# One-core attention with a feed-forward block: step order, PSUM banks and instruction ranks read from stored tables

## The chip, the core and the metric

The kernel runs on one core of one Trainium2 chip. A core has TensorE (PE, matmuls and transposes), VectorE (DVE), ScalarE (ACT), GpSimd (POOL) and SyncE (SP, which here issues every DMA). Matmul results land in PSUM, eight banks, from where DVE and ACT read them. The metric is the device time of one execution in microseconds (us); of several runs the median counts.

## What is computed

Batch 4, 8 heads, 768 positions, head size 64; model width 512, inner width 2048. All inputs are float32 in memory.

```python
k_sum = k.reshape(B, H, nb, 32, D).max(axis=3)            # 24 blocks of 32 keys
v_sum = v.reshape(B, H, nb, 32, D).mean(axis=3)
scores_l = scale * q @ k.T, kept where |i - j| < 16, else -1e9
scores_s = scale * q @ k_sum.T + log(32)
a = softmax(concat([scores_l, scores_s]))                 # with 1e-9 on the sum
x = a @ concat([v, v_sum])                                # heads side by side: [B, S, 512]
xn = (x - mean) / sqrt(var + 1e-6) * g_ln
out = x + relu(xn @ w_ch1) @ w_ch2
```

## The kernel before

The 3072 rows are cut into 24 tiles of 128. A tile's attention is done in two half steps of four heads each (t = 0 to 47). The first 12 half steps (batch 0) work on float32 data: `early_qk` makes scores (tile name `s`), `softmax` takes on DVE the masked scores with their minimum (`p`, `mn`) and on ACT the exponentials, `early_transp` transposes on PE (`pp`, copied to `pT`), `early_pv` multiplies by the values (`o`). Later half steps work on pairs of fp16 numbers. `ln` and `lnT` normalize and transpose a tile (`xn`, `xs`).

The feed-forward part runs on pairs of tiles (groups of 256 rows), each float32 product split into three fp16 ones. Its 32 weight blocks of 512 KB each are fetched (`fetch_w`, tile `raw`), decoded on DVE by three instructions (`dec_w`: `wf<-raw`, `wf<-raw,wf`, `raw<-raw,wf`), squared and summed on ACT, scaled by a common power of two per set of blocks (`scale_w`, six times: a tiny matmul, tile `wps`, sums over partitions) and split into fp16 halves on ACT and DVE (`conv_w`, tile `wp`). Only then can `g1` (12 matmuls a piece into `h`, then `hh` on ACT and `hl` on DVE) and `g2` (6 matmuls a piece into `a`) use them. From row group 5 on, `sp1`, `sp2` and `sw2` do the same by a scheme with fewer products (tiles `qx`, `qy`, `qz`, `a_x`, `a_y`).

For batches 1 to 3, statistics are loaded through a few staging buffers (`bst`, `qs`, `qw`): `batch_k` (block maxima `kmax`), `batch_q`, `batch_v` (block sums `vsum`); each buffer is loaded, reduced on DVE, reduced on ACT and then loaded again.

Nothing is issued while the steps are called. A `Plan` records each operation with what it must wait for, then `issue` (line 439) orders all 3593 recorded operations by a list scheduler with built-in costs (`schedule`, line 300, `improve`, `search`) and writes them out engine by engine. Lines 457 and 460 are where every instruction of the trace is issued, so tiles rather than lines tell them apart. Three things settle the order before: the order in which the body calls the steps decides who uses a rotating buffer first; `LOADS` (line 64) fixes the first DMA issues on SP by hand; PSUM tiles alternate between the two banks of their kind (`psum`, line 475: kinds s, o, h, a). Where the scheduler expects PE to wait long, it puts transposes of the identity there as fill (`spare`).

Of the kernel before, what the change touches and what calls it, by code (L numbers as in the profile page):

```python
# [104 lines left out]
class Plan:  # L105
# [12 lines left out]
    def __init__(self):  # L118
        self.ops, self.slots, self.prev, self.uses = [], {}, {}, {}
        self.joined, self.opens, self.closes = False, None, ()  # L120
        self.names, self.stage = [("", ())], 0
        for e in self.ENGINES:
            setattr(self, e, Plan.Queue(self, e))
# [7 lines left out]

    def step(self, f):


        def call(*a):
            outer, self.stage = self.stage, len(self.names)
            self.names.append((f.__name__, a))
            f(*a)
            self.stage = outer

        return call

# [296 lines left out]
    def issue(self, nc):  # L439
        for x in self.ops:  # L440
            x.first = in_front(self.names[x.stage], x.engine)
        self.watch()
        after = [self.waits(x) for x in self.ops]
        then = [[] for _ in after]
        for i, x in enumerate(after):
            for j, wait in x:
                then[j].append((i, wait))
        rank = [0.0] * len(after)
        for i in reversed(range(len(after))):
            x = self.ops[i]  # L450
            rank[i] = min((rank[j] for j, _ in then[i]), default=0.0) - x.busy - x.moving - self.WAIT[x.engine]
        best = self.search(rank, after, then)
# [12 lines left out]
def body(ctx: ExitStack, tc, qt, qa, qe, kt, ks, va, vb, vs, g_ln, w1, w2, blocks, out):  # L465
# [3 lines left out]
    pools = {n: ctx.enter_context(tc.tile_pool(name="ps" + n, bufs=1, space=bass.MemoryType.PSUM)) for n in "soha"}  # L469
    banks = dict.fromkeys("soha", 0)  # L470

# [92 lines left out]

    turn = {}

    def home(kind):
        n = turn[kind] = turn.get(kind, -1) + 1
        return HOMES[kind][n % len(HOMES[kind])]

    stg_n = [0]

    def stg(tag, shape, dt=F32):
        stg_n[0] += 1
        if tag == "bst1":
            tag = ("bst", "qs")[stg_n[0] % 2]
        elif tag in ("bst", "qs"):
            tag = home(tag)
        return work(tag, f"{tag}{stg_n[0]}", shape, dt, 1 + (tag == "xn"))

# [3 lines left out]
    @pl.step  # L584
    def batch_k(b, hp):
        if hp == 0:
            bt["m", b] = work("kmax" if b else "ksum", f"kmax{b}", [P, 4, NB], F32, 1 + (b == 0))
            if b:
                bt["a", b] = work("vabs", f"vabs{b}", [P, 3, 8])
                nc.gpsimd.memset(bt["a", b][:], 0.0)  # L590
        m = bt["m", b]
        n = 2 if b else 1
        for c in range(n):
            cs = slice(NB // n * c, NB // n * (c + 1))
            if b:
                kk = stg("bst1" if b == 1 else "bst", [P, NB // n, BLK])[:]
# [55 lines left out]
    def batch_v(b, c):  # L652
        if c == 0:
            bt["v", b] = work("vsum", f"vsum{b}", [96, P], F32, 1)
        t, ab = bt["v", b], bt["a", b]
        vv = stg("bst1" if b == 1 else "bst", [96, 16, BLK])
        nc.sync.dma_start(vv[:], vs[b, c])
# [5 lines left out]
    @pl.step  # L663
    def batch_q(b, c):
        x = stg("bst1" if b == 1 else "bst", [P, DM])
        nc.sync.dma_start(x[:], qa[b, :, c * DM : c * DM + DM])
        nc.scalar.activation(x[:], x[:], AF.Abs, accum_out=bt["a", b][:, 1, c : c + 1])
# [43 lines left out]
    def load_q(t):  # L711

        T, hh = divmod(t, 2)
        qs = stg('qs', [P, 4, P])
        for half in range(2):
# [8 lines left out]
    def load_k(t, pr):  # L724
        T, hh = divmod(t, 2)
        b = T // NT
        at = home("ksg")
        ksg = late[at] if at in late else work(at, f"ksg{t}_{pr}", [P, 2, NC])
# [3 lines left out]
        )  # L732
        at = home("kh")
        kh = work(at, f"kh{t}_{pr}", [P, 2, NC], F16) if at else late["kh"]
# [64 lines left out]
    def transp(t):  # L799

        p = st[t, "p"]
        p16 = work(home("p16"), f"p16_{t}", [P, 4, 3, P], F16)
        first, rest, last = (p16[:, :, i] for i in range(3))
# [3 lines left out]
        nc.gpsimd.tensor_tensor(last[:, :, D:], p[:, :, P:], last[:, :, :D], ALU.subtract)  # L807
        pT = work(home("pT"), f"pT_{t}", [P, 12, P], F16)
        nc.sync.dma_start_transpose(pT[:], p16.rearrange("p j i k -> p (j i k)"))
# [120 lines left out]
    def ln(T):  # L930
# [7 lines left out]
        nc.gpsimd.tensor_tensor(rs[:], rs[:], mhalf[:], ALU.pow)  # L938
        xn = stg("xn", [P, DM])
        if XA <= T < XE:  # L940
# [190 lines left out]
    def combine2(u):  # L1131

        top, low = (wt[2, rows2(u, j)] for j in range(2))
        yt, yb = (stg("xn", [P, DM]) for _ in range(2))
        for y, w in ((yt, top), (yb, low)):
# [317 lines left out]
    for t in range(8, 2 * TT + 1):  # L1453
# [30 lines left out]
        if t % 2:  # L1484
            norm(t // 2)
    with tc.manual_schedule():
        pl.issue(tc.nc)
# [54 lines left out]
```

## Time and profile before

| | |
|---|---|
| median of 3 runs | 611.51 us (608.76 to 613.46) |
| span of the profiled execution | 609.7 us |
| PE busy | 592.2 us, 97% |
| DVE busy | 520.5 us, 85% |
| ACT busy | 434.9 us, 71% |
| POOL busy | 235.9 us, 39% |
| DMA queue of SP | 95.04 MB, 63.3% of 16 engines |
| chain that ended last | PE 74%, DVE 14%, DMA 6% |

Matmuls are pipelined, so a PE that counts as busy may hide short waits; the spacing of matmul starts tells more. The shares are averages over stages with different limits, so the stretches have to be read one by one. Idle time of an engine that nothing waits for costs nothing.

### The profile page before, as it was taken

What the parts mean: (1) busy time and instruction counts of PE and PEld (TensorE: products, weight loads), DVE (VectorE), ACT (ScalarE), POOL (GpSimd) and SP (SyncE); (2) the same over time, 40 slices, a digit from 0 to 9 for tenths busy, and PEclk for the clock granted to TensorE, in tenths of its full rate; (3) what the DMA queues carried; (4) which work ended last, traced back from release to release, by engine and by line L of the source; (5) the groups of instructions that cost most, each with busy time, mean ns of one, the idle gap of its engine ahead of it and who ended that gap; (6) DMA issues with size and microseconds to landing.
All of it is one profiled execution on the core that took longest, in us unless ns stands there. A gap on an engine that the chain in (4) does not pass through costs nothing.

```text
span 609.7 us, 16537 instructions
## 1 busy us (share of the span) xinstructions
PE 592.2 (97%) x6097; PEld 448.4 (74%) x6097; DVE 520.5 (85%) x1351; ACT 434.9 (71%) x968; POOL 235.9 (39%) x447
## 2 busy tenths in 40 slices
PE   6998899989999999999999999999999999999997
PEld 4687776675677688677687867877685896987976
DVE  3799998899989989998999978678999999868435
ACT  2798798778889877669698857657867777544221
POOL 5131221123856675575354433317553532410000
PEclk8999999999999999999999999999999999999999
DMA  9990478624899995578899868736446673531101
GB/s 260 366 329 15 124 236 298 206 66 122 215 260 234 206 193 147 120 148 194 189 212 231 190 142 172 140 88 152 107 114 138 144 178 73 103 75 34 47 1 35
DMA packets 138176, 96.09 MB, mean 158 GB/s; under 512 B 96112, under 2 KB 120944, under 8 KB 138096
## 3 DMA queue, kind: packets, MB, share of 16 engines
q1 hardware_dynamic: 138096, 95.04, 63.3%
q8 instruction: 48, 0.79, 0.6%
q14 instruction: 32, 0.26, 0.1%
HBM read 66.27 MB, written 6.29 MB: 119 GB/s over the span
## 4 chain that ended last, share of the span: by engine, by line
PE 74%; DVE 14%; DMA 6%; ACT 2%; issue 2%; POOL 1%; SPq 0%; ACTq 0%; DVEq 0%; POOLq 0%
PE a L460 30%; PE qx L460 11%; PE h L460 11%; PE qz L460 6%; PE o L460 4%; PE s L460 4%; PE qy L460 3%; DVE wf L460 3%; PE a_x L460 3%; PE a_y L460 2%; DVE wp L460 2%; DVE raw L460 2%; DVE hl L460 2%; DVE p L460 1%; DMA k<-in_ks 1%
## 5 line engine op out<-in xcount | busy, mean ns | idle before, releaser
L460 PE MATMUL a<-wp,hh 128*128 128x512 f16 x640 | 190.4, 379 | 0.0
L460 PEld LDWEIGHTS <-wp 128*128 128x128 f16 x1968 | 152.0, 98 | 19.1 <-issue 2.0
L460 PE MATMUL a<-wp,hl 128*128 128x512 f16 x320 | 121.3, 379 | 0.0
L460 PE MATMUL h<-xs,wp 128*128 128x256 f16 x960 | 112.4, 273 | 0.4 <-DVE xs L460 0.4
L460 PEld LDWEIGHTS <-hh 128*128 128x128 f16 x736 | 68.9, 98 | 56.9 <-issue 0.2
L460 POOL TENSOR_TENSOR p<-p,p 128x512 f16<-128x512 f32 x72 | 75.8, 1058 | 61.0 <-ACT p L460 37.6
L460 PEld LDWEIGHTS <-wd 128*128 128x128 f16 x1176 | 70.7, 98 | 5.5
L460 ACT ACTIVATE p<-p,mn,sv 128x184 f32<-128x184 f32 x144 | 67.4, 529 | 7.7 <-POOL mn L460 7.5
L460 PEld LDWEIGHTS <-hl 128*128 128x128 f16 x368 | 36.0, 98 | 39.1 <-DVE hl L460 0.8
L460 POOL TENSOR_SCALAR mn<-mn,sv 128x2 f32<-128x2 f32 x72 | 33.2, 464 | 58.8 <-DVE mn L460 57.7
L460 DVE CUSTOM_DVE_ANT_0 p<-s,mask 128x184 f32<-128x184 f32 x144 | 43.1, 340 | 5.0 <-PE s L460 4.5
L460 PE MATMUL qx<-xs,wp 128*128 128x128 f16 x672 | 42.9, 219 | 0.1
L460 POOL TENSOR_SCALAR rs<-mv 128x1 f32<-128x1 f32 x24 | 8.9, 372 | 64.7 <-DVE mv L460 60.7
L460 ACT ACTIVATE v<-vst,sv 128x512 f16<-128x512 f32 x36 | 25.8, 719 | 11.2 <-PE o L460 9.6
L460 DVE SCALAR_TENSOR_TENSOR x<-a,wsc,x 128x512 f32<-128x512 f32 x40 | 29.7, 742 | 4.7 <-PE a L460 4.6
L460 ACT CAST p<-p 128x512 f16<-128x512 f32 x72 | 33.4, 506 | 0.2
L460 DVE SCALAR_TENSOR_TENSOR v<-vst,sv,v 128x512 f16<-128x512 f32 x36 | 31.4, 873 | 1.6 <-ACT v L460 1.6
L460 DVE SCALAR_TENSOR_TENSOR hl<-h,hh 128x512 f16<-128x512 f32 x40 | 27.0, 681 | 3.8 <-ACT hh L460 3.7
L460 ACT ACTIVATE hh<-h 128x512 f16<-128x512 f32 x40 | 23.5, 586 | 8.2 <-PE h L460 8.1
L460 PEld LDWEIGHTS <-pT 128*128 128x128 f16 x720 | 26.0, 98 | 2.5
L460 PE MATMUL o<-v,pT 128*128 128x65 f16 (+1 forms) x720 | 27.7, 193 | 0.0
L460 PEld LDWEIGHTS <-qhl 128*128 128x128 f16 x288 | 23.5, 98 | 3.3
(235 smaller groups left out, 1355.5 us busy)
## 6 DMA issues: line engine op xcount, KB each, us to landing
raw<-in_w SPq DMA_DIRECT2D x32, 512.0 KB
ksg<-in_kt SPq DMA_DIRECT2D x48, 184.0 KB
out_x<-x SPq DMA_DIRECT2D x20, 256.0 KB
qw<-in_qt SPq DMA_DIRECT2D x36, 128.0 KB
vst<-in_va SPq DMA_DIRECT2D x36, 128.0 KB
qs<-in_qt SPq DMA_DIRECT2D x36, 128.0 KB
keys<-in_kt SPq DMA_DIRECT2D x24, 184.0 KB
vst<-in_vb SPq DMA_DIRECT2D x80, 32.0 KB
```

The lines of the kernel that those rows point to most:

```text
L460: getattr(getattr(nc, self.ops[i].engine), op)(*a, **k)
```

## The change

No operation is added or removed: the same 3593 operations are recorded. What changes is what decides their order and their place.

- `step` now only collects calls; `record_steps` records them in the order of the stored table `ORDER` (621 steps), so rotating buffers may be taken in another order.
- `psum` takes the bank of each tile from `BANKS`, one digit for one of all eight banks, instead of alternating within a kind.
- `issue` takes one rank per operation from `RANKS` and runs the scheduler once with them; the search over starts is left out. `LOADS` is empty.
- Buffers that were chosen by a running count (`home`, `stg`) are now chosen by the number of the load (`stage_in`, `rows`).

```diff
+ORDER = (
+    "#)#&#,#'#7$Z###($e#+#9#;#:#<#%#D#3#8#-$k$[$l#5#6#$#4$c$h#1#2#*#=#>#?#@#A#W#B#C#l#E#F#X#G#H#I#J#K#L$f$]$_$v#M#N"
...
+BANKS = (
...
+RANKS = (
...
+LOADS = []
...
     def step(self, f):
+        return lambda *a: self.steps.append((f, a))
+
+    def record_steps(self):
+        order = decode(ORDER) or range(len(self.steps))
+        assert len(order) == len(self.steps)
+        for i in order:
+            f, a = self.steps[i]
+            self.stage = len(self.names)
             self.names.append((f.__name__, a))
             f(*a)
...
+        rank = decode(RANKS)
+        if not rank:
...
+        else:
+            best = self.improve(rank, after, then, 1)[0]
...
     def psum(tag, name, shape, at=None):
-        if at is None:
+        if BANKS:
+            tag, at = "s0s1o0o1h0h1a0a1"[2 * int(BANKS[len(turns)]) :][:2]
+            turns.append(at)
+        elif at is None:
             at = banks[tag] = 1 - banks[tag]
...
+    def stage_in(b, n, shape):
+        tag = home("bst", n) if b > 1 else ("qs", "bst")[n % 2]
+        return work(tag, f"in{b}_{n}", shape)
```

Where the rows stand is what the tables decide. The first place is SP's queue, from the last of the four key loads on (`k_3`; `qw` is a query tile, `vw` and `vend` values, `vst` value tails, `blk` and `gcol` constants, `raw` a weight block of 512 KB). Before:

```order
L460 DMA k_3_93<-in_ks 128x768
L460 DMA blk<-in_blocks 128x144
L460 DMA vw_100<-in_va 128x4x128 x2
L460 DMA vw_101<-in_va 128x4x128 x2
L460 DMA vw_102<-in_va 128x4x128 x2
L460 DMA vend<-in_vb 32x2x256
L460 DMA vst_77<-in_vb 32x2x128 x2
L460 DMA raw_252<-in_w 128x1024
L460 DMA raw_253<-in_w 128x1024
L460 DMA qw_95<-in_qe 128x512
L460 DMA raw_254<-in_w 128x1024
```

The same place after the change:

```order
L561 DMA k_3_93<-in_ks 128x768
L561 DMA qw_94<-in_qe 128x512
L561 DMA vw_100<-in_va 128x4x128
L561 DMA blk<-in_blocks 128x144
L561 DMA raw_112<-in_w 128x1024
L561 DMA vw_102<-in_va 128x4x128
L561 DMA qw_95<-in_qe 128x512
L561 DMA vw_100<-in_va 128x4x128
L561 DMA gcol<-in_g_ln 128x4x1
L561 DMA raw_128<-in_w 128x1024
L561 DMA raw_129<-in_w 128x1024
L561 DMA raw_107<-in_w 128x1024
```

The first weight block moved from behind all seven value loads to behind one of them, and three more blocks stand where one stood.

The second place is PE, from the end of the first scores on (`v` sums the value blocks of batch 0, `s_0` and `s_1` are the scores of the next half step, `pp` the transposes of the first one's probabilities). Before:

```order
L460 MATMUL s_1_111<-kx,qw_94 128x192
L460 MATMUL v_109<-vw_100,blk 120x512 x2
L460 MATMUL s_0_120<-ident 128x128
L460 MATMUL s_0_120<-kx,qw_94 128x184
L460 MATMUL s_1_121<-kx,qw_94 128x184
L460 MATMUL s_0_120<-kx,qw_94 128x192
L460 MATMUL s_1_121<-kx,qw_94 128x192
L460 MATMUL v_109<-vw_101,blk 120x512 x2
L460 MATMUL v_109<-vw_102,blk 120x512 x2
L460 MATMUL v_109<-vend,blk 120x512
L460 MATMUL pp_0_113<-ident,p 128x128 x3
```

After the change, from the second half step's last scores on (`qw_95` belongs to half steps 2 and 3):

```order
L561 MATMUL s_1_132<-kx,qw_94 128x192
L561 MATMUL pp_0_120<-ident,p 128x128 x3
L561 MATMUL pp_1_123<-ident,p 128x128 x3
L561 MATMUL s_0_146<-ident 128x128
L561 MATMUL s_0_146<-kx,qw_95 128x184
L561 MATMUL s_1_147<-kx,qw_95 128x184
L561 MATMUL s_0_146<-kx,qw_95 128x192
L561 MATMUL s_1_147<-kx,qw_95 128x192
L561 MATMUL pp_0_134<-ident,p_89 128x128 x3
L561 MATMUL v_116<-vw_100,blk 120x512
```

The scores of half steps 1 and 2 now stand ahead of the first value product instead of behind two and seven of them. Of the 70 fill transposes before (35 of them behind half step 5, the others later), 28 are left, all between the second and the third value product.

On DVE, the first instruction that decodes the first weight block moved ahead of the second half step's masked scores, and the sixth `wps` matmul, which is the last of its kind in both orders, stands behind 269 DVE instructions that it needs instead of 285.

## Rows read from the trace of the kernel before

**Rows 1.** The page: busy time of each engine, share of the span, instructions.
```profile
PE 592.2 (97%) x6097; PEld 448.4 (74%) x6097; DVE 520.5 (85%) x1351; ACT 434.9 (71%) x968; POOL 235.9 (39%) x447
```

**Rows 2.** 20 us stretches: us busy of PE, PEld, DVE, ACT, POOL; clock, DMA, GB/s.
```profile
20.00:40.00 20.00, 19.39 (x158) 16.11 (x157) 17.52 (x71) 18.71 (x52) 3.90 (x16) 1.00 1.03 386
40.00:60.00 20.00, 17.08 (x146) 14.77 (x147) 19.83 (x57) 17.12 (x47) 4.91 (x11) 1.00 0.24 72
...
140.00:160.00 20.00, 20.00 (x121) 11.42 (x119) 19.68 (x52) 18.84 (x41) 10.08 (x19) 1.00 0.55 155
```

**Rows 3.** Longer stretches, same columns.
```profile
0.00:140.00 140.00, 126.21 (x936) 96.35 (x937) 119.89 (x347) 106.86 (x293) 34.99 (x115) 0.99 0.65 211
140.00:300.00 160.00, 160.00 (x1396) 113.20 (x1394) 148.83 (x389) 131.63 (x282) 98.56 (x154) 1.00 0.81 184
```

**Rows 4.** Instructions on PE in order: start us, length us, what, [idle before <-releaser].
```profile
7.55 0.91 PE L460 MATMUL s<-kx,qw 64*128 64x184 f32 x8
11.66 3.63 PE L460 MATMUL v<-vw,blk 128*120 128x512 f32 x4 [3.21 <-DVE mn L460]
...
15.33 0.91 PE L460 MATMUL s<-kx,qw 64*128 64x184 f32 x8
16.17 3.69 PE L460 MATMUL v<-vw,blk 128*120 128x512 f32 x8
...
134.84 0.34 PE L460 MATMUL wps<-wacc,ones 128*128 128x8 f32 x2
...
606.25 0.27 PE L460 MATMUL a_x<-lone,hl 128*128 128x256 f16 x1
```

**Rows 5.** Instructions on DVE in order of time, same columns.
```profile
10.38 0.35 DVE L460 CUSTOM_DVE_ANT_0 p<-s,emask 128x192 f32<-128x192 f32 x1
...
16.39 0.36 DVE L460 CUSTOM_DVE_ANT_0 p<-s,emask 128x192 f32<-128x192 f32 x1 [4.84 <-PE s L460]
...
17.66 0.43 DVE L460 TENSOR_SCALAR wf<-raw 128x512 uint32<-128x512 uint32 x1
...
19.46 0.42 DVE L460 TENSOR_SCALAR wf<-raw 128x512 uint32<-128x512 uint32 x1
...
22.80 0.35 DVE L460 CUSTOM_DVE_ANT_0 p<-s,msk 128x184 f32<-128x184 f32 x1 [1.46 <-PE s L460]
...
104.17 0.68 DVE L460 TENSOR_REDUCE vsum<-qs 96x16 f32<-96x512 f32 x1 [1.68 <-DMA qs<-in_vs]
...
110.08 0.68 DVE L460 TENSOR_REDUCE vsum<-qs 96x16 f32<-96x512 f32 x1
```

**Rows 6.** The first weight loads on SP's queue, same columns.
```profile
12.41 0.89 SPq L460 DMA_DIRECT2D raw<-in_w  x2
```

**Rows 7.** The fill transposes: count, ns min/median/max, first and last start.
```profile
L457 PE MATMUL spare<-ident x69: 272/273/305, 41.7 to 71.6; 128*128 128x128 f32 x69
```

**Rows 8.** DVE's waits between 72 and 135 us: us in total, times, longest.
```profile
DVE vsum L460 <- DMA qs<-in_vs: 1.7, 1, 1.7
DVE vsum L460 <- DMA bst<-in_vs: 1.4, 1, 1.4
```

**Rows 9.** The stretches around PE's first wait, columns as in the 20 us stretches.
```profile
8.00:12.00 4.00, 0.80 (x7) 0.53 (x5) 3.00 (x10) 2.28 (x8) 1.45 (x15) 0.95 1.18 308
12.00:16.00 4.00, 4.00 (x13) 1.59 (x12) 0.00 (x0) 0.25 (x1) 0.00 (x0) 0.62 1.11 279
```

**Rows 10.** DVE between 140 and 300 us by form: busy us, mean ns | idle before.
```profile
L460 DVE SCALAR_TENSOR_TENSOR kl<-keys,sv,kh 128x368 f16<-128x368 f32 x11 | 9.1, 824 | 0.1
...
L460 DVE SCALAR_TENSOR_TENSOR kl<-ksg,sv,kh 128x368 f16<-128x368 f32 x11 | 7.0, 634 | 0.5 <-PE s L460 0.5
```

**Rows 11.** PE's waits between 140 and 606 us: us in total, times, longest.
```profile
PE a_y L460 <- DVE hl L460: 0.5, 1, 0.5
```

**Rows 12.** DVE up to 140 us by form: busy us, mean ns | idle before.
```profile
L460 DVE SCALAR_TENSOR_TENSOR hl<-h,hh 128x512 f16<-128x512 f32 x15 | 10.1, 681 | 0.0
...
L460 DVE TENSOR_REDUCE kmax<-bst 128x12 f32<-128x384 f32 x6 | 3.3, 543 | 0.0
```

More of the change, by code (lines that the diff above doesn't have):

```diff
@@ L57, with decode @@
+def decode(text):
+    n = [ord(c) - 35 - (c > "\\") for c in text]
+    return [90 * a + b for a, b in zip(n[::2], n[1::2])]
 SEQ = [(1 + m // 8 % 2, m % 8 + m // 16 * 8) for m in range(2 * NF)]
@@ L120, in __init__ @@
         self.joined, self.opens, self.closes = False, None, ()
-        self.names, self.stage = [("", ())], 0
+        self.names, self.stage, self.steps = [("", ())], 0, []
         for e in self.ENGINES:
@@ L447, in issue @@
                 then[j].append((i, wait))
[L448 to L452, printed above, removed]
+        rank = decode(RANKS)
+        if not rank:
+            rank = [0.0] * len(after)
+            for i in reversed(range(len(after))):
+                x = self.ops[i]
+                rank[i] = min((rank[j] for j, _ in then[i]), default=0.0) - x.busy - x.moving - self.WAIT[x.engine]
+            best = self.search(rank, after, then)
+        else:
+            best = self.improve(rank, after, then, 1)[0]
         self.time, self.start, self.end, fills = best
@@ L469, in body @@
     pools = {n: ctx.enter_context(tc.tile_pool(name="ps" + n, bufs=1, space=bass.MemoryType.PSUM)) for n in "soha"}
-    banks = dict.fromkeys("soha", 0)
+    banks, turns = dict.fromkeys("soha", 0), []
     def work(tag, name, shape, dt=F32, bufs=1):
@@ L563, in go_late, with home, rows @@
         late["kh"] = room[:, DM : DM + NC].bitcast(F16).rearrange("p (u c) -> p u c", u=2)
-    turn = {}
-    def home(kind):
-        n = turn[kind] = turn.get(kind, -1) + 1
+    def home(kind, n):
         return HOMES[kind][n % len(HOMES[kind])]
[L571 to L579, printed above, removed]
+    def stage_in(b, n, shape):
+        tag = home("bst", n) if b > 1 else ("qs", "bst")[n % 2]
+        return work(tag, f"in{b}_{n}", shape)
+    def rows(name):
+        return work("xn", name, [P, DM], F32, 2)
     bt = {}
@@ L595, in batch_k @@
             if b:
-                kk = stg("bst1" if b == 1 else "bst", [P, NB // n, BLK])[:]
+                kk = stage_in(b, 2 * hp + c, [P, NB // n, BLK])[:]
                 nc.sync.dma_start(kk, ks[b, hp, :, cs])
@@ L655, in batch_v @@
         t, ab = bt["v", b], bt["a", b]
-        vv = stg("bst1" if b == 1 else "bst", [96, 16, BLK])
+        vv = stage_in(b, 14 + c, [96, 16, BLK])
         nc.sync.dma_start(vv[:], vs[b, c])
@@ L664, in batch_q @@
     def batch_q(b, c):
-        x = stg("bst1" if b == 1 else "bst", [P, DM])
+        x = stage_in(b, 8 + c, [P, DM])
         nc.sync.dma_start(x[:], qa[b, :, c * DM : c * DM + DM])
@@ L713, in load_q @@
         T, hh = divmod(t, 2)
-        qs = stg('qs', [P, 4, P])
+        qs = work(home("qs", t), f"qs{t}", [P, 4, P])
         for half in range(2):
@@ L801, in transp @@
         p = st[t, "p"]
-        p16 = work(home("p16"), f"p16_{t}", [P, 4, 3, P], F16)
+        p16 = work(home("p16", t), f"p16_{t}", [P, 4, 3, P], F16)
         first, rest, last = (p16[:, :, i] for i in range(3))
@@ L807, in transp @@
         nc.gpsimd.tensor_tensor(last[:, :, D:], p[:, :, P:], last[:, :, :D], ALU.subtract)
[L808 removed]
+        pT = work(home("pT", t), f"pT_{t}", [P, 12, P], F16)
         nc.sync.dma_start_transpose(pT[:], p16.rearrange("p j i k -> p (j i k)"))
@@ L938, in ln @@
         nc.gpsimd.tensor_tensor(rs[:], rs[:], mhalf[:], ALU.pow)
-        xn = stg("xn", [P, DM])
+        xn = rows(f"xn{T}")
         if XA <= T < XE:
@@ L1133, in combine2 @@
         top, low = (wt[2, rows2(u, j)] for j in range(2))
-        yt, yb = (stg("xn", [P, DM]) for _ in range(2))
+        yt, yb = (rows(f"y{u}{n}") for n in "tb")
         for y, w in ((yt, top), (yb, low)):
```

96 lines of the change are left out of this document (89 added, 7 removed).

## The prediction, made before the changed kernel was run

> **What bounds the kernel now.** The busy line of the page comes first [rows 1]: PE is busy 97% of the span, so whatever an order can win is among the other 3% and what the busy time hides. The stretches say where that is. Up to 140 us PE is busy 126.2 of 140 us; from 140 to 300 us it is busy 160 of 160 [rows 3], and between 140 and 606 us its list of waits has one entry, of 0.5 us [rows 11]. So there are two kernels: one of 140 us with holes on PE, and one of 470 us in which PE never stops and in which an order can win almost nothing. The reader should look only at the first.
>
> In that part PE is not what limits. DVE is busy 19.8 of 20 us between 40 and 60 us, while PE is busy 17.1 [rows 2], and even that holds 69 transposes that only fill time, between 41.7 and 71.6 us [rows 7] (one more opens the fill). DVE decodes and splits 32 weight blocks there beside its attention work, and PE waits for what it makes. But DVE itself starts late. It takes the first half step's scores at 10.38 us, then waits 4.84 us for the second's, decodes the first weight block only at 17.66 us, and waits 1.46 us more for the third's scores at 22.80 us [rows 5]. The rows on PE say why: behind the first scores stands the value product `v`, which waits and then takes 3.63 us for four passes, and the second scores, though only 0.91 us long, come behind it, at 15.33 us; five more value products (3.69 us for the first eight passes) stand ahead of the third [rows 4]. The decoding is late because the first two weight loads are issued at 12.41 us [rows 6], behind all the values.
>
> So I measure the kernel at one landmark, the sixth and last `wps` matmul, at 134.84 us. The last matmul starts at 606.25 us [rows 4], 471.4 us later, of which about 1.1 are waits (the 0.5 listed, the rest hidden in the busy time). What comes behind, 3.4 us to the end of the span of 609.7 us, is a store that both kernels end with. Whatever the landmark gains, the span gains, if PE stays without holes.
>
> **The change, part by part.** No operation is added or taken away, so each term is an instruction that stands elsewhere.
>
> 1. *Work ahead of the landmark on PE.* I counted it from the order. Before: 29 pieces of `g1`, 14 of `g2`, 24 `pp`, 24 `o`, 12 `s` and the seven value products. After: the same, but 16 of `g2`, 22 `pp`, 22 `o`, 11 `s`. At the spacing of starts (1.3 us a piece, 0.33, 0.7, 0.84) that is +2.6 -0.7 -1.4 -0.8: 0.3 us less, nothing. PE does the same by then. The fill falls from 70 to 28 transposes, but a fill stands where PE would wait anyhow, so I cost it at nothing: it is the wait's length that counts, and that is DVE's.
>
> 2. *Work ahead of the landmark on DVE.* Before, 285 instructions lie ahead of the last one it needs; after, 269. Behind it now: four masked scores (0.27 us each in a row), two `kmax` of the next batch (0.46), two `vsum` (0.6), two `hl` (0.6), one normalization's statistics (0.6) and six short ones (0.5 in all); one more 0.66 us addition stands ahead. A row is about 0.08 us longer than the spacing, since neighbours overlap [rows 12]. Sum: 1.1 + 0.9 + 1.2 + 1.2 + 0.6 + 0.5 - 0.7 = **4.8 us less** (of 114 before). DVE has to do them later, behind the landmark, where it has 11 idle us in 160 [rows 3].
>
> 3. *DVE's start.* The second half step's scores now stand ahead of every value product, and the first weight load behind one value load instead of seven. Bounds: if both are always there in time, DVE loses none of the 4.84, 1.46 and the 0.4 us of small gaps up to 22.80: 6.7 us gained. [...] DMA should keep up: by the shapes in the order, 2.7 MB are asked for up to the first weight block where it was 4.1, and the queue moves 0.3 to 0.4 MB a us [rows 2, 9], so that block is there 4 us earlier, near 13 us, and each of the next (0.52 MB, 1.4 to 1.7 us) about as fast as DVE decodes one (1.8 us, 17.66 to 19.46 [rows 5]). I take **4.5 us**, nearer to the full gain than to none, because DVE has decoding to do whenever scores are late.
>
> 4. *Staging buffers.* Batch 1's statistics pass through two buffers, and DVE waited 1.7 and 1.4 us for their loads [rows 8]. One round (reduce, ACT, load again) took 5.9 us, 104.17 to 110.08 [rows 5]. After the change the last five rounds of each buffer are 5.1 to 5.7 us of DVE work apart, where most were 5.6 to 7.3: up to 5 x 0.8 = 4 us of waits in place of 3.1. Bounds: 2 us gained (ACT is quicker, 71% busy) to 5 lost. I take **1 lost**.
>
> 5. *Behind the landmark.* A few pieces later the new order needs DVE results with 1.5 us less PE work in front of them than at the landmark (a `g1` piece behind 111.8 us of DVE work, 109.5 of PE work with fill). Before, that difference did not grow. **1.5 lost.** The 0.5 us wait of `a_y` [rows 11] goes, since another group's piece now stands there; I leave as much for new waits among 470 us of PE work whose banks have all moved: nothing, bounds 0.5 gained to 3 lost.
>
> 6. *Banks and buffers.* A tile may take any of eight banks. Where PE waits for DVE that gives nothing; it is what lets steps 2 and 3 stand so. Nothing of its own.
>
> Sum: 4.8 + 4.5 - 1.0 - 1.5 = 6.8 us, so the landmark comes at about 128 us and the span is **602.9 us**. The profiled execution (609.7 us) lies a little under the median of the runs (611.51 us); in proportion that makes **604.5 us**.
>
> **The rivals.**
>
> *PE's clock stays low at the start.* [...] Time: 609.7 - 6.8 + 2.5 = 605.4, or 607 us as a median. Chance 0.15.
>
> *The staging buffers take it back.* Step 4 at 5 lost and step 3 at 2: 609.7 - (4.8 + 2 - 5 - 1.5) = 609.4, as a median 611. Against it: DVE has other work to put between. Chance 0.15. That the tables do nothing at all is out: the order shows the moves.
>
> *Everything in time.* Steps 3 and 4 at their good ends: 4.8 + 6.7 + 2 - 1.5 = 12, a span of 597.7, as a median 599.5. For it: each piece alone fits. Chance 0.14.
>
> *Slower: DVE becomes the bound after 140 us.* At 140 us of PE work DVE stood 5.4 us ahead of need by work count, and stands 1.6 ahead after the change: 3.8 us of reserve gone. Between 140 and 300 us DVE is idle 11.2 us [rows 3], and the 32 `kl` vary by source, 634 against 824 ns [rows 10]. If none of the idle time can be squeezed and all `kl` take 0.19 us more, 11.2 + 6.1 - 3.8 = 13.5 us of PE waits arise, 6.7 us more than is gained: a span of 616.4, a median of 618. It decides from 3.8 us on. Against it: most of that idle time is DVE waiting for ACT and PE because it is early. [...] Chance 0.08.
>
> **How the numbers follow.** Forecast 0.48 (600.5 to 608.5 by itself), then 0.15, 0.15, 0.14, 0.08. The range leaves out the last and the outer parts of two others: 598 to 612 us. One per cent, about what a measurement of this kernel can tell from no change, is 6.1 us: faster is below 605.4, slower above 617.6. Faster: 0.14, most of the forecast (0.38) and a little of the clock's case (0.04), 0.56. Slower: 0.08. Within: 0.36.
>
> **What would show it.** The second half step's scores start near 12 us and DVE's first `wf<-raw` near 12 to 13 us instead of 17.66: step 3. The sixth `wps` near 128 us, PE's spacing solid from there: steps 2 and 5. Waits of `vsum` or `kmax` on `bst` and `qs` above 4 us: step 4 too small. A clock under 1 beyond 16 us: the first rival. The forecast falls if PE's list of waits between 140 and 606 us, now 0.5 us, is several us long.

## The result, and the profile after

The changed kernel takes 606.86 us (median of ten runs, 602.15 to 612.93) against 611.03 us (608.76 to 613.46) of the kernel before on the same chip. The ratio is 0.9906, with a 95% interval of 0.9878 to 0.9934; it leaves out the run of 612.93 us, which was disturbed; the mean of the other nine is 605.5 us. So the change gains 0.7 to 1.2%, about 5.7 us. The profiled execution spans 604.7 us, 5.0 less than before; 6.8 were forecast.

The page of the changed kernel: busy time of each engine, its share of the span, instructions. PE loses 4.1 us of busy time [rows 1], which the 42 fill transposes fewer account for, roughly (27 in a row take 3.11 us, so 42 some 4.8 by estimate); DVE's share rises.

```profile
PE 588.1 (97%) x6055; PEld 446.3 (74%) x6055; DVE 523.9 (87%) x1351; ACT 435.7 (72%) x968; POOL 231.8 (38%) x447
```

Stretches of the changed kernel, then two of the kernel before, cut at each one's landmark, the sixth `wps` matmul: length, us busy of PE, PEld, DVE, ACT, POOL, granted clock, DMA share, GB/s.

```profile
0.00:40.00 40.00, 33.76 (x208) 25.96 (x209) 30.29 (x98) 26.41 (x73) 14.13 (x68) 0.91 0.99 339
40.00:126.31 86.31, 82.99 (x641) 63.45 (x640) 81.54 (x219) 73.86 (x200) 12.82 (x35) 1.00 0.52 169
140.00:300.00 160.00, 158.48 (x1360) 110.94 (x1359) 151.20 (x395) 134.14 (x298) 99.30 (x156) 1.00 0.83 200
```

```profile
0.00:40.00 40.00, 34.37 (x224) 25.79 (x224) 26.04 (x101) 24.98 (x69) 12.54 (x69) 0.96 0.99 331
40.00:134.84 94.84, 86.73 (x679) 67.24 (x679) 89.70 (x234) 80.21 (x220) 20.28 (x43) 1.00 0.52 165
```

These four rows up to the landmark hold the gain. By 40 us DVE has done 30.29 us of work where it had done 26.04: a start 4.2 us better. Up to the landmark it has 30.29 + 81.54 = 111.8 us to do where it was 115.7: 3.9 less. Its idle time from 40 us to the landmark is 4.8 where it was 5.1. Together that is 8.5 us. From 140 to 300 us PE is no longer busy throughout: 1.5 us are missing [rows 3].

The changed kernel on PE in order of time, where [rows 4] stood: start us, length us, what, [idle before <-releaser].

```profile
10.20 0.91 PE L561 MATMUL s<-kx,qw 64*128 64x184 f32 x8
...
13.21 0.91 PE L561 MATMUL s<-kx,qw 64*128 64x184 f32 x8
...
25.67 1.11 PE L561 MATMUL v<-vend,blk 32*120 32x512 f32 x2 [0.92 <-DMA vend<-in_vb]
...
27.96 0.46 PE L561 MATMUL o<-vst,pT 128*128 128x130 f32 x2 [0.70 <-ACT vst L561]
...
126.31 0.29 PE L561 MATMUL wps<-wacc,ones 128*128 128x8 f32 x2
...
601.21 0.27 PE L561 MATMUL a_x<-lone,hl 128*128 128x256 f16 x1
```

The landmark is 8.53 us earlier (126.31, was 134.84). The last matmul starts 474.90 us behind it, where it was 471.41: 3.49 us of the gain are given back there. All that follows is about these two numbers.

DVE of the changed kernel, same columns, where [rows 5] stood: the first decode at 11.42 us (was 17.66) and the third half step's scores at 14.26 (was 22.80), with no wait listed between them.

```profile
11.42 0.43 DVE L561 TENSOR_SCALAR wf<-raw 128x512 uint32<-128x512 uint32 x1
11.76 0.34 DVE L561 CUSTOM_DVE_ANT_0 p<-s,msk 128x184 f32<-128x184 f32 x1
...
14.26 0.35 DVE L561 CUSTOM_DVE_ANT_0 p<-s,msk 128x184 f32<-128x184 f32 x1
```

DVE's waits up to 40 us, of the changed kernel and then of the kernel before: us in total, times, longest.

```profile
DVE kmax L561 <- DMA k<-in_ks: 4.4, 3, 2.9
DVE rc L561 <- PE o L561: 1.2, 1, 1.2
DVE wf L561 <- ACT vst L561: 1.0, 1, 1.0
DVE p L561 <- POOL k L561: 0.9, 1, 0.9
...
DVE wf L561 <- DMA raw<-in_w: 0.7, 1, 0.7
DVE p L561 <- PE s L561: 0.3, 1, 0.3
```

```profile
DVE p L460 <- PE s L460: 6.3, 2, 4.8
DVE kmax L460 <- DMA k<-in_ks: 5.6, 2, 3.0
...
DVE wf L460 <- ACT wf L460: 0.6, 2, 0.4
DVE p L460 <- ACT pT L460: 0.2, 1, 0.2
```

The two waits for scores, 6.3 us, are down to 0.3; 1.2 less for the first keys and 0.8 of small ones come to it. Against that stand four waits that were not there: for `o`, for ACT's `vst`, for the keys from POOL and for `raw`, 3.8 us in all. That leaves the 4.2.

PE's waits between 140 and 606 us in the changed kernel (us in total, times, longest), where [rows 11] had one of 0.5 us:

```profile
PE h L561 <- DVE mn L561: 1.5, 1, 1.5
PE qy L561 <- DVE hl L561: 0.9, 1, 0.9
PE qx L561 <- DMA ksg<-in_kt: 0.8, 1, 0.8
PE qz L561 <- DVE hl L561: 0.2, 1, 0.2
```

They come to 3.4 us, and one of 0.4 stands just behind the landmark; that is 3.3 more than before, nearly all of the 3.49 lost. (The third is put down to a load. But ACT's copy `one` ends at 397.08 us, 0.05 us before that matmul starts, and e10 and e11 name `one` for it.) The longest can be followed back. The rows of the load, ACT, DVE and PE around it, columns as above:

```profile
161.16 0.53 SPq L561 DMA_DIRECT2D in<-in_qa  x1
...
165.18 0.63 ACT L561 ACTIVATE in<-in 128x512 f32<-128x512 f32 x1 [2.12 <-DMA in<-in_qa]
...
168.80 0.69 DVE L561 SCALAR_TENSOR_TENSOR hl<-h,hh 128x512 f16<-128x512 f32 x1 [1.90 <-ACT hh L561]
...
172.86 1.47 PE L561 MATMUL h<-xs,wp 128*128 128x256 f16 x12 [1.52 <-DVE mn L561]
```

ACT stands at `in<-in`, a reduction of batch 2's statistics, because its load, issued at 161.16 us, is not there. Behind it in ACT's order stand the copies `hh` on which DVE's `hl` waits, and behind `hl` the masked scores whose PSUM bank the next piece `h` takes. A load that PE doesn't need for a long time has held up three engines, one after the other. At 313 us the same happens with a `vsum` of batch 3 (1.08 us on DVE, 0.88 on PE's `qy`).

### The profile page after: what moved, and what is told of

The parts are those of the page before. It is cut to its first block, busy times and chain, and to the rows that moved or that the text cites. A ratio compares the mean times of both kernels' runs of the same rounds, so it can differ in the third digit from the quotient of the medians.

```text
span 604.7 us, 16441 instructions
## 1 busy us (share of the span) xinstructions
PE 588.1 (97%) x6055; PEld 446.3 (74%) x6055; DVE 523.9 (87%) x1351; ACT 435.7 (72%) x968; POOL 231.8 (38%) x447
## 4 chain that ended last, share of the span: by engine, by line
PE 70%; ACT 9%; DMA 9%; DVE 8%; issue 2%; SPq 1%; POOL 1%; ACTq 0%; DVEq 0%
PE a L561 26%; PE qx L561 11%; PE h L561 10%; PE qz L561 6%; PE o L561 4%; DMA raw<-in_w 4%; PE a_x L561 3%; PE s L561 3%; PE qy L561 3%; PE a_y L561 3%; DMA in<-in_vs 2%; ACT p L561 2%; ACT wp L561 2%; ACT wf L561 1%; DMA in<-in_ks 1%
## 5 line engine op out<-in xcount | busy, mean ns | idle before, releaser
L561 PE MATMUL h<-xs,wp 128*128 128x256 f16 x960 | 111.1, 273 | 3.0 <-DVE mn L561 1.5
L561 POOL TENSOR_TENSOR p<-p,p 128x512 f16<-128x512 f32 x72 | 72.5, 1014 | 41.3 <-ACT p L561 36.3
L561 POOL TENSOR_SCALAR mn<-mn,sv 128x2 f32<-128x2 f32 x72 | 37.8, 528 | 50.8 <-DVE mn L561 48.9
L561 ACT ACTIVATE in<-in 128x384 f32<-128x384 f32 (+2 forms) x66 | 38.7, 587 | 15.7 <-DVE kmax L561 6.9
L561 POOL COPY ksg<-ksum 128x48 f32<-128x48 f32 x48 | 17.5, 366 | 33.1 <-DMA ksg<-in_kt 24.5
L561 ACT ACTIVATE xn<-x,mv,rs 128x512 f32<-128x512 f32 x20 | 16.2, 810 | 17.6 <-POOL mv L561 17.5
```

## The experiments

All but e7, e8 and e10 change the order of a few instructions in the finished plan of the changed kernel (e4: of the kernel before); e6 and e9 also change a buffer. No operation is added or left out, but for fills. Pieces of the resulting order stand for the edit. "Behind" is the time from the landmark to the start of the last matmul: 471.41 us before, 474.90 after.

### e10: the changed kernel once more

The same kernel, beside the runs of e8.

> The changed kernel itself, once more, beside the others on the same chip. If runs are told apart by the clock at the start, those with a mean clock of 0.997 and above take 602 to 604 us and those of 0.994 and below 605 to 609; ratio 0.988 to 0.993 as a whole.

603.29 us (601.34 to 607.88, five runs), ratio 0.9872 (0.9849 to 0.9895). Together with the nine above the changed kernel has a mean of 605.0 us over fourteen runs. The profiled execution has its landmark at 123.32 us, 3 us earlier than in the first, and 479.30 us pass behind it. Its longest wait and the stretches around it (columns as in the stretches above):

```profile
PE h L561 <- DVE mn L561: 3.4, 1, 3.4
```

```profile
168.00:172.00 4.00, 0.65 (x6) 0.40 (x4) 3.78 (x13) 4.00 (x11) 2.79 (x4) 0.84 0.45 120
172.00:176.00 4.00, 4.00 (x36) 3.07 (x35) 4.00 (x7) 3.33 (x9) 3.90 (x8) 0.50 0.90 204
176.00:180.00 4.00, 4.00 (x21) 2.29 (x20) 2.28 (x5) 2.73 (x7) 2.83 (x6) 0.81 0.40 124
```

It is the wait of the chain above: here ACT stood 3.66 us for the load, DVE 3.43, PE 3.35. PE's clock was then 0.50 for four microseconds and 0.81 for the next four, and the twelve `h` matmuls behind the wait took 2.72 us, where they took 1.47 at 1.00 in the first execution. So by estimate a wait of 3.4 us cost about 6 (3.4, half of 4 us, and a fifth of the next 4). The load itself:

```profile
158.32 0.53 SPq L561 DMA_DIRECT2D in<-in_qa  x1
```

The earlier landmark is not what makes the wait longer, since the issue of the load moves with it (34.85 us behind the landmark in the first execution, 35.00 here). The load took longer: ACT's reduction starts 4.0 us after the issue there and 5.7 us after it here (164.03). Why it took longer stays open.

By 40 us DVE has done 32.01 us of work in this execution, 6.0 more than before, where the first had 4.2 more; PE's clock is 1.00 up to 40 us.

### e3: the early loads of before

Nine loads (the second query tile, the five value loads behind the first, `vend` and two `vst`) go back ahead of the first weight block; all engines keep their new order. SP's queue:

```diff
-DMA raw_112<-in_w 128x1024
-DMA vw_102<-in_va 128x4x128
 DMA qw_95<-in_qe 128x512
 DMA vw_100<-in_va 128x4x128
+DMA vw_101<-in_va 128x4x128 x2
+DMA vw_102<-in_va 128x4x128 x2
+DMA vend<-in_vb 32x2x256
+DMA vst_77<-in_vb 32x2x128 x2
+DMA raw_112<-in_w 128x1024
```

> The changed kernel with its first loads as in the kernel before: all seven value loads and the two value tails ahead of the first weight block; TensorE, VectorE, ScalarE and GpSimd keep the changed order. Theory early weights: VectorE's first wf comes at 15 to 16 us instead of 11.4, it stands ahead of masked scores in VectorE's order, so VectorE is idle some 3 to 4 us more by 20 us and the sixth wps comes 2 to 4 us later: ratio 0.994 to 0.998. Rival full queue: the 16 DMA engines are busy 1.0 of the time from 8 to 40 us whatever the order, and the waits for vend and vst go, so nothing is lost: ratio 0.985 to 0.991.

612.3 us (608.28 to 614.82, twelve runs), ratio 1.0017 (0.9995 to 1.0038): the whole gain is gone. DVE, in order of time:

```profile
17.35 0.43 DVE L580 TENSOR_SCALAR wf<-raw 128x512 uint32<-128x512 uint32 x1 [6.27 <-DMA raw<-in_w]
```

The decode stands ahead of the scores now, so the late load holds up both. The stretches, columns as above:

```profile
0.00:40.00 40.00, 29.92 (x168) 21.68 (x168) 25.43 (x80) 21.96 (x61) 11.65 (x63) 0.87 0.98 335
40.00:130.90 90.90, 87.61 (x681) 67.42 (x681) 86.16 (x237) 78.41 (x212) 15.25 (x40) 1.00 0.50 162
```

By 40 us DVE has done 25.43 us, 0.6 less than before. The load is the first reason (6.27 us); PE's clock of 0.50 from 16 to 24 us came behind it, and what it added was not separated. Up to the landmark it has 111.6 us to do, 4.1 less. So e3 has less work ahead of the landmark, as the changed kernel, and not the start, and its landmark comes at 130.90 us, 3.9 earlier. But behind it 476.64 us pass, 5.2 more than before, with the same three waits on PE as in the changed kernel, longer (2.7, 1.8 and 0.8 us). They make up that loss, and the first two stand behind staged loads again: ACT stood 3.12 us for batch 2's, DVE 1.97 us for batch 3's. So e3 does not show that the work put behind the landmark has to be paid for there; e3 with the moves of e11 was not run. What the change keeps over e3 is DVE's start.

### e4: the early start alone, in the kernel before

Two weight loads, the second and third scores and their transposes go forward; everything else stays.

```diff
 MATMUL s_1_111<-kx,qw_94 128x192
-MATMUL v_109<-vw_100,blk 120x512 x2
 MATMUL s_0_120<-ident 128x128
...
-DMA vw_100<-in_va 128x4x128 x2
+DMA vw_100<-in_va 128x4x128
+DMA raw_252<-in_w 128x1024
+DMA qw_95<-in_qe 128x512
+DMA vw_100<-in_va 128x4x128
+DMA raw_253<-in_w 128x1024
```

> The kernel before with the early part of the change alone: on the load queue the first two weight blocks and the second query tile move up behind one and two value loads, on TensorE the scores of half steps 1 and 2 (and the transposes of half step 0's probabilities, which the latter need) move ahead of the value products. Theory start: the first wf comes at 12 to 13 us instead of 17.66, the third half step's masked scores near 17 instead of 22.8, the sixth wps 4 to 5 us earlier (near 130.5), and as nothing behind it is moved the span falls by as much: 605 to 606, ratio 0.991 to 0.994. Rival: the staging buffers or the full load queue give it back before the landmark: span 608 to 610, ratio 0.997 to 1.000.

613.57 us (611.92 to 616.76, twelve runs), ratio 1.0047 (1.0026 to 1.0069): slower. DVE's rows:

```profile
19.13 0.35 DVE L479 CUSTOM_DVE_ANT_0 p<-s,msk 128x184 f32<-128x184 f32 x1 [2.68 <-PE s L479]
...
27.74 0.16 DVE L479 TENSOR_SCALAR rc<-o 128x4 f32<-128x4 f32 x1 [6.76 <-PE o L479]
```

DVE starts early (first decode at 12.79 us) and then stands 6.76 us at `rc`, which needs PE's first `o`, and that stands behind all the value products, which now start later. PE's clock also fell (0.68 from 16 to 20 us and 0.67 from 24 to 28, where it was 1.00 before), which delays `o` too; the two were not separated within the 6.76 us. A low clock on the whole does not explain the result: the three runs with a mean clock of 1.000 take 611.95 to 613.18 us, where the kernel before, beside it, takes 609.05 to 610.70 at 1.000. The landmark falls back to 138.09. In the changed kernel DVE's order has decoding, which needs no values, where `rc` stood. So loads, PE order and DVE order belong together: neither part alone (e3, e4) gains.

### e1: more fill

22 more fill transposes keep PE busy where its clock had fallen.

```diff
+MATMUL spare<-ident 128x128 x10
 MATMUL v_116<-vend,blk 120x512
 MATMUL wps_0_182<-wacc,ones 128x4
+MATMUL spare<-ident 128x128 x8
 MATMUL o_122<-ident 128x128
...
+MATMUL spare<-ident 128x128 x4
 MATMUL pp_1_151<-ident,p 128x128 x3
```

> The changed kernel with 22 more fill transposes on TensorE and nothing else: 10 ahead of the last value product, 8 ahead of the first o of half step 0, 4 ahead of the third half step's pp, where it waited 0.92, 0.70 and 0.48 us; behind these waits its granted clock was 0.73 at 28 to 30 us, 0.50 to 0.57 from 30 to 36 us. Theory clock: the low level behind those waits costs the span about 3 us. Then the clock is 1.00 from 28 to 36 us, the scores at 31 us take 0.91 us instead of 1.62, VectorE's wait of 1.2 us for o at 36 us goes, the sixth wps comes near 123 us and the median is 602 to 604 (ratio to the kernel before 0.985 to 0.988). Rival: what is late there is loads and VectorE, and a slow TensorE fits into its waits: 606 to 608, ratio 0.990 to 0.993.

604.32 us (602.66 to 607.56, six runs), ratio 0.99 (0.9865 to 0.9936). The profiled execution has a clock of 1.00 throughout, and its landmark at 125.01 us, 1.3 earlier than the first execution of the changed kernel and 1.7 later than e10's; behind it 473.59. Against the 605.0 us of the changed kernel that is no difference that these runs can tell.

### e8: no fill

The changed kernel without its 28 fill transposes.

> The changed kernel without its 28 fill transposes (17.6 to 20.8 us); nothing else differs. The changed kernel's own runs go with their mean granted clock: 602.2 us at 1.000, 603.4 at 0.997, 604.2 to 607.3 at 0.994 to 0.996, 607.3 to 608.4 at 0.991 to 0.992. Theory clock: TensorE, left idle from 17.6 to 21 us, falls to the low level earlier and stays there through the value products and the first o; mean clock 0.985 to 0.990 and a median of 609 to 612, ratio 0.996 to 1.002. Rival: the mean clock only marks executions whose early loads come late; then a lower clock alone costs little, median 606 to 608, ratio 0.990 to 0.994.

606.26 us (603.78 to 608.33, six runs), ratio 0.9923 (0.9896 to 0.9949). Two stretches, columns as above:

```profile
16.00:20.00 4.00, 1.24 (x6) 0.44 (x4) 4.00 (x11) 3.25 (x11) 1.60 (x3) 1.00 1.12 340
20.00:24.00 4.00, 3.46 (x6) 1.57 (x7) 3.78 (x11) 2.57 (x7) 0.00 (x0) 0.74 1.06 364
```

Behind the hole the clock falls, where the changed kernel has 1.00, yet the landmark is at 122.94 us, no later than in the two profiled executions with the fill (126.31 and 123.32). DVE is busy 7.78 of these 8 us, and has done 32.4 us of work by 40 us: while it has decoding to do, PE may be slow here. The fill is worth some 1 us in time (means of 606.1 and 605.0), within the spread.

### e2: the last values earlier

`vend` and two `vst` loads go ahead of two weight blocks.

```diff
+DMA vend<-in_vb 32x2x256
+DMA vst_77<-in_vb 32x2x128 x2
 DMA raw_166<-in_w 128x1024
 DMA raw_213<-in_w 128x1024
-DMA vend<-in_vb 32x2x256
-DMA vst_77<-in_vb 32x2x128
```

> The changed kernel with three small loads (vend, 64 KB, and the two of vst for half step 0) ahead of two weight blocks of 512 KB on the load queue instead of behind them; all other orders unchanged. Theory clock: TensorE's waits of 0.92 us for vend and 0.70 us for vst go, so the clock stays at 1.00 behind 28 us and VectorE waits about 0.3 us more for the raw block at 23.8 us: median 602 to 604, ratio 0.985 to 0.988. Rival: the weight blocks are what VectorE lives on, each later load costs as much as is won: 606 to 608, ratio 0.990 to 0.993.

603.98 us (602.04 to 608.67, six runs), ratio 0.9893 (0.9859 to 0.9928); landmark 124.13. The wait for `vend` is gone; PE's `v` now waits 1.8 us for `vw` and DVE 2.1 for `raw`. The DMA share is 1.00 up to 40 us; here the loads that went forward made others late. These runs tell no difference in time from the changed kernel.

### e6: a third staging buffer

`qw1` takes three of batch 1's loads (`if b == 1 and n in (14, 17, 21)`), `in_14` is loaded earlier, and a load of batch 2 that held the buffer moves behind.

```diff
 DMA in_5_384<-in_ks 128x384
+DMA in_14_401<-in_vs 96x512
 DMA raw_337<-in_w 128x1024
```

> The changed kernel with a third staging buffer for three of the eight value-sum loads of batch 1 (numbers 14, 17 and 21 go through qw1, which stands unused until then), the first of these loads issued five places earlier, and one early load of batch 2 that held this buffer moved behind; nothing else is moved. Theory staging: VectorE's wait of about 1.9 us for a vsum near 109 us goes and the sixth wps comes 1 to 2 us earlier than 126.3: span 603, ratio 0.987 to 0.990. Rival: the wait moves to the next staged load or weight block, VectorE's waits for loads between 72 and 135 us stay at 3.5 to 4.5 us in all and nothing is gained: ratio 0.990 to 0.993.

604.51 us (603.95 to 606.28, four runs), ratio 0.991 (0.9888 to 0.9932). DVE's waits for these loads fall from 3.5 to 2.8 us in all, the landmark is at 123.70. No gain in time that can be told.

### e5: work that PE needs ahead of what waits

Two masks ahead of `hl`, an addition ahead of `vsum`, two `hl` and a copy earlier. Two pieces:

```diff
+ISA p_378,mn_485<-s_0_483,mask_436 128x184
+ISA mn_485 128x1
 SCALAR_TENSOR_TENSOR hl_500<-h_498,hh_499 128x512
...
+SCALAR_TENSOR_TENSOR hl_1_781<-qx_1_768,hh_1_780 128x512
 TENSOR_REDUCE vsum_962<-in_21_1046 96x16
-SCALAR_TENSOR_TENSOR hl_1_781<-qx_1_768,hh_1_780 128x512
```

> The changed kernel with six operations moved behind the landmark, five on VectorE and one on ScalarE, each of them ready and standing behind something that is not: two masked scores of half step 15 ahead of two hl (TensorE's h waits 1.5 us for them at 172.9 us), one x ahead of two vsum (0.4 us at 127.8), two hl of sp1 ahead of a vsum that waits for its load and of a qy (0.9 us at 314.4, 0.2 at 319.4), one copy of sp1 ahead of three exponentials (0.75 us at 397.1). All of these TensorE waits are for a result that frees a PSUM bank or feeds the next product, on engines that are not full there. Theory order: they are the 3.5 us that the changed kernel loses behind the landmark; then TensorE's waits from 128 us on fall from 3.8 us to under 1, from the landmark to the last matmul it takes 471.5 to 472 us instead of 474.9, and the ratio to the kernel before falls from 0.9906 to about 0.985. Rival VectorE is full there: the waits come back at the next pieces, 474 to 475 us, ratio 0.989 to 0.992.

607.86 us (603.9 to 610.02, nine runs), ratio 0.9937 (0.9906 to 0.9968). The wait at 172 us is gone, but `pp` loses about 0.9 in three pieces near 132 us (by the spacing of starts), `qx` waits 0.9 and 0.6, two others 0.3 and 0.2; behind the landmark 474.24, 0.7 better. Moving work on DVE leaves the load in place: ACT, a step ahead, still stands 1.40 us for it, with the staged reduction in front of its copies. This points at ACT's order; e11 tests it.

### e9: e1, e2, e6 and three of e5's moves together

> The changed kernel with what helped in a profile put together: 22 more fill transposes before 31 us, vend and vst ahead of two weight blocks, the third staging buffer, two masked scores of half step 15 and one x moved ahead on VectorE. If the gains add, the clock stays at 1.00, the sixth wps comes at 121 to 123 us, TensorE's waits behind it fall by 1.5 us and the median is 600 to 602, ratio 0.982 to 0.986. If each is only the same late early loads seen from another side, 603 to 605, ratio 0.988 to 0.991.

605.48 us (604.8 to 609.24, seven runs), ratio 0.993 (0.9906 to 0.9955): the gains do not add up. The wait at 172 us is gone, and a longer one stands at 313: `qy` waits 2.0 us on `hl`, behind batch 3's staged `vsum`, and the clock falls to 0.58 behind it. Another new one, of `h`, takes 1.5 us near 257. Behind the landmark 478.68.

### e11: the staged reductions behind what PE waits for

Three moves at the cause: ACT's reduction of `in_12` behind two copies `hh`, DVE's `hl` ahead of the last `vsum` of batch 3, ACT's copy `one` ahead of its reduction.

```diff
-ACTIVATE in_12_635,vabs_613<-in_12_635 128x512
 ACTIVATE hh_509<-h_508 128x512
...
 ACTIVATE hh_499<-h_498 128x512
+ACTIVATE in_12_635,vabs_613<-in_12_635 128x512
...
+SCALAR_TENSOR_TENSOR hl_1_781<-qx_1_768,hh_1_780 128x512
 TENSOR_REDUCE vsum_962<-in_21_1046 96x16
...
+COPY one_0_858<-qx_0_855 128x512
 ACTIVATE in_21_1046,vabs_948<-in_21_1046 96x512
```

> The changed kernel with three operations moved so that no staged load of batches 2 and 3 stands ahead of work that TensorE waits for: on ScalarE the reduction of batch 2's query block (in_12) goes behind the hh of g1 piece 16, four places on; on VectorE the hl of sp1 goes ahead of batch 3's last vsum, on ScalarE the copy one of sp1 ahead of that block's reduction. Theory staged loads: in seven profiles of this order ScalarE waits 1.5 to 3.7 us for in_12, VectorE then 0.23 us less for hh, TensorE 0.35 to 3.35 us for the masked scores behind it, and 0.6 to 2.0 us for the sp1 piece near 312 us. Both TensorE waits go whatever the load takes: none above 0.3 us at 165 to 175 and at 310 to 317 us, from the sixth wps to the last matmul 472 to 473 us instead of 473.6 to 479.3, median 601.5 to 603.5 (all undisturbed runs of the changed kernel: mean 605.0), ratio 0.985 to 0.988. Rival VectorE is full: the waits come back at the pieces behind, 474.5 us and more, ratio 0.989 to 0.992.

603.6 us (602.47 to 605.24, six runs), ratio 0.987 (0.9842 to 0.9897). Both waits are gone. PE's waits from 140 to 606 us, and the stretch of 140 to 300:

```profile
PE qx L580 <- ACT one L580: 0.7, 1, 0.7
PE qz L580 <- DVE hl L580: 0.3, 1, 0.3
PE qz L580 <- PE s L580: 0.2, 1, 0.2
```

```profile
140.00:300.00 160.00, 160.00 (x1377) 111.85 (x1376) 152.25 (x397) 135.30 (x302) 98.66 (x156) 1.00 0.82 200
```

PE is busy throughout again, and behind the landmark 472.13 us pass: 2.8 of the 3.5 us lost are back. The landmark of this execution was late (127.78), behind a clock of 0.77 to 0.81 at 28 to 36 us and a wait of `pp` near 117 us. A late landmark is not what removed the waits: in e12, which has the same moves, it comes at 125.07, earlier than in the first execution of the changed kernel, and both waits are gone there, too. That shows the chain to be the cause of the waits. In time the gain is not told apart: e11's ratio of 0.987 is that of e10, the changed kernel as it is.

### e12: the same for batch 1

e11, and four masks and four exponentials ahead of batch 1's first staged `vsum` and reduction.

```diff
+ISA p,mn_361<-s_0_359,msk 128x184
...
 TENSOR_REDUCE vsum_400<-in_14_401 96x16
...
+ACTIVATE p<-p,mn_361 128x184
...
 ACTIVATE in_14_401,vabs_186<-in_14_401 96x512
```

> The kernel of the run before (staged loads of batches 2 and 3 moved behind) with the same done once ahead of the landmark: on VectorE the four masked scores of half step 10 go ahead of batch 1's first vsum, on ScalarE their four exponentials ahead of that block's reduction. Theory staged loads: VectorE's wait for this vsum (1.7 to 2.0 us) shrinks by the 1.1 us of masked scores that now stand in it, TensorE's waits for the exponentials near 117 us (1.05 us in the changed kernel, 1.85 in the run before) go, and the sixth wps comes about 1 us earlier than it would (it lies between 122.9 and 127.9 us by the state of the early loads): median 602 to 603, ratio 0.984 to 0.987. Rival: the next staged loads or weight blocks take the time back: VectorE's waits for loads from 72 to 128 us stay at 4 us and more, ratio 0.987 to 0.990.

603.42 us (602.78 to 604.37, four runs), ratio 0.9876 (0.9857 to 0.9894). DVE's waits for staged loads between 72 and 127 us, in the changed kernel and then in e12:

```profile
DVE vsum L561 <- DMA in<-in_vs: 2.4, 2, 1.9
DVE kmax L561 <- DMA in<-in_ks: 1.1, 2, 0.6
```

```profile
DVE kmax L580 <- DMA in<-in_ks: 0.7, 2, 0.5
DVE vsum L580 <- DMA in<-in_vs: 0.6, 1, 0.6
```

The landmark is at 125.07 us in spite of a clock of 0.57 from 28 to 36 us; behind it 473.27, with waits of 0.8, 0.5 and 0.5 us on PE. In time it equals e11. Against the fourteen runs of the changed kernel (605.0) the two are some 1.4 us better, and no run lies above 605.3 where those reach 608.4; so few runs cannot tell that for certain, and against the runs of the kernel before beside it e10 does as well (0.9872). It is faster than the kernel before by 1.1 to 1.4%, and without the two long waits.

### e7: order and banks kept, ranks searched

`RANKS = ""`, so the search of the kernel before ranks the new steps.

> The changed kernel without its stored ranks: order of the steps and PSUM banks stay as stored, and the ranks of the operations come from the search of the kernel before. One part of the change undone. If the gain sits in the stored order and banks, the sixth wps stays near 126 to 128 us and the ratio near 0.99. If it sits in the ranks (which decide what stands ahead on VectorE), the landmark comes at 133 us or later and the ratio is 1.0 to 1.02.

617.11 us (616.05 to 619.23, four runs), ratio 1.0123 (1.0097 to 1.015). The landmark keeps 7.3 of the 8.5 us (127.50), but behind it 482.96 pass, with these waits on PE:

```profile
PE qz L513 <- ACT seven L513: 3.9, 1, 3.9
PE a_y L513 <- DVE hls L513: 2.1, 1, 2.1
```

So with the new recording order and its banks a search for ranks finds most of the landmark's gain, too; the stored ranks keep PE without holes as long as these behind it. Stored ranks with the old order of steps were not run (one number belongs to each operation of the new order), nor another bank for the one piece that waits at 172 us.

## Why the prediction held, and where its steps were off

The sign came out, and the time (605.0 us as the mean of fourteen runs, 606.9 as the first median, for a forecast of 604.5). The first median lies within one per cent of the kernel before, to which the prediction gave 0.36; the mean of fourteen lies below 605.4, to which it gave 0.56. In the profiled execution 5.0 us were gained where the sum had 6.8: step by step it was off by -0.9, -0.3, +1.4 and -2.0 us (steps 2 to 5), so errors of both signs partly cancelled, and that the total came so near is in part luck. These sizes are of one execution. In e10's, 11.5 us were gained at the landmark and 7.9 lost behind it.

The sum has a slip of its own. Step 5 is a loss behind the landmark, but the landmark "at about 128 us" has it subtracted already. By steps 2 to 4 alone it comes at 126.5 us; 126.31 was measured.

- **Step 1**, PE's work and the fill at nothing: right. e8 puts the fill at some 1 us, within the spread.
- **Step 2**, 4.8 us less DVE work ahead of the landmark: 3.9 measured (4.2 in e10's execution). e3, which has this term and not the start, ends no earlier than the kernel before, but it loses the time in the waits of step 5. With these waits gone, only 0.7 us more pass behind the landmark than before in e11 and 1.9 in e12.
- **Step 3**, DVE's start, 4.5: 4.2 measured, 6.0 in e10's execution. The rows named came earlier than forecast (second scores 10.20 for 12, first decode 11.42 for 12 to 13). Nearly the full gain was there (6.0 us of waits for scores), and new waits took a part back. That loads, PE and DVE must move together was not said; e3 and e4 show that neither part alone gains.
- **Step 4**, staging, 1 lost: the wrong sign. DVE's idle time from 40 us to the landmark fell by 0.4 us instead. `vsum` and `kmax` waited 3.5 us, under the 4 that would have shown it wrong, against 3.1 [rows 8]; other small waits went.
- **Step 5**, behind the landmark: 1.5 lost for DVE results that come later against PE's work, and nothing for new waits, with bounds of 0.5 gained to 3 lost. In all 3.5 were lost, and this is the step that failed. The first term was too large: only 0.4 us of waiting stands just behind the landmark. The second was the loss: 3.1 us, just beyond its bound, and 7.5 in e10's execution. The `a_y` wait went as said. The new waits were put at nothing because PE had 470 us without holes; what was not looked at are the loads that stand in ACT's and DVE's orders there. The order showed the staged reduction ahead of the copies; the trace before showed that such loads come 1.4 to 1.7 us late [rows 8]. Put together they give a wait of that order (ACT's was 2.12 us). e11 takes it away, and 2.8 us less are lost behind the landmark.
- **Step 6**, banks give nothing of their own: not separated from the order (e7 keeps both). At 172 us the bank of a masked score is what ties PE's piece to DVE.

The sign by which the forecast was to fall, PE's list of waits several us long, came true in part: 3.4 us. The span was off by 1.8 us (604.7 for 602.9): steps 2 to 4 together came out 0.2 us better than their sum, and step 5 took 2.0 more.

**The rivals.** *The clock*: it fell, though only from 28 us on, behind the waits for `vend` (0.92 us) and `vst` (0.70):

```profile
28.00:30.00 2.00, 2.00 (x13) 1.82 (x13) 2.00 (x5) 1.87 (x6) 0.00 (x0) 0.73 1.07 392
30.00:34.00 4.00, 3.83 (x19) 3.05 (x19) 3.68 (x14) 3.33 (x10) 0.55 (x2) 0.50 0.97 340
34.00:36.00 2.00, 2.00 (x12) 1.93 (x11) 0.89 (x4) 0.99 (x3) 0.95 (x3) 0.57 1.01 387
```

Its 607 us is near the first median. No run shows the 2.5 us that it adds for a low clock at the start, nor the 2 us at which the next rival has step 3: 4.2 us came there, with a clock of 1.00 up to 28 us. Some cost may lie at 28 to 36 us: DVE waits 1.22 us for `o` at 36 us, a wait that e10's execution, with a clock of 1.00, does not have. Not every wait of PE had a low clock behind it: behind 3.30 us in e8 it was 0.74, behind 3.35 in e10 0.50 and behind 2.0 in e9 0.58, but behind 2.67 us in e3 the twelve `h` matmuls took 1.47 us, as at 1.00. What a low clock cost differed: some 1 us in time, within the spread, at 20 to 28 us in e8, where DVE has decoding to do; over 2 us by estimate at 172 in e10, where PE limits. At 28 to 36 us the runs point both ways: the changed kernel has its landmark at 126.31 us with the low clock and at 123.32 without, but e12, at 0.57, has it at 125.07, and e1, at 1.00, at 125.01. Over the fourteen runs the time goes with the mean clock (601.3 to 602.2 us at 1.000, 603.0 to 604.5 at 0.997, 604.2 to 608.4 at 0.991 to 0.996), but e1, four times at 1.000, has 602.7 to 604.7. With the low clock at 28 us PE's waits for `vend` and `vst` ahead of it were longer, too (0.92 and 0.70 us, where e10's execution has 0.5 and 0.4), and late loads and a low clock were not told apart.

*Staging takes it back*: no, as said at step 4; its bill came behind the landmark. *Everything in time*: the best runs (601.3 us) come near its 599.5. *DVE becomes the bound*: no. DVE is still idle 8.8 us from 140 to 300, and its three kinds of `kl`, by mean ns, are on the whole no slower than before (two of them are in [rows 10]; the third took 655 ns before and takes 604; all together they take 22.7 us for 32 before and 24.0 for 34):

```profile
L561 DVE SCALAR_TENSOR_TENSOR kl<-keys,sv,kh 128x368 f16<-128x368 f32 x11 | 9.2, 833 | 0.0
L561 DVE SCALAR_TENSOR_TENSOR kl<-ksg,sv,kh 128x368 f16<-128x368 f32 x12 | 8.2, 685 | 0.0
```

The waits for DVE that did arise were of its order, not of how much it has to do. What the spread of `kl` comes from, no run here shows.

## What to carry to other kernels

Where one engine limits the start, look for what it could do before its first wait, and move its loads, its own order and the order of the engine that feeds it together: parts of it alone gained nothing here. A landmark that comes earlier is not yet time gained; count what waits behind it, too. And in an engine's order, look at every instruction that waits for a load which nobody needs soon: here 2.12 us of such a wait on ACT came back as 1.90 us on DVE and 1.52 on PE.

## What was not expected of the hardware

Two executions of one and the same program differ by 3 us at the landmark (126.31, 123.32) and by 4.4 us behind it (474.90, 479.30). Behind it one and the same load, issued at the same place in the order, kept ACT waiting 2.12 or 3.66 us. The kernel before, with no such wait, varies less (a standard deviation of 1.3 us over the 67 runs beside the experiments, 2.4 us over the fourteen of the changed kernel). Behind one wait of 3.35 us in the middle of the kernel, with PE busy on both sides of it, the clock was 0.50 for the next four us. And 28 fill transposes that kept the clock at 1.00 from 20 to 28 us (0.74 and 0.83 without them) were worth no more than about 1 us in time.
